# Five loads of K issued from GpSimd over part of the DMA engines, in an attention backward for one query

## The chip, the cores and the metric

The kernel runs on one core of a Trainium2 chip. The core has TensorE (PE in the profile, its weight loads PEld), VectorE (DVE), ScalarE (ACT), GpSimd (POOL) and SyncE (SP), and sixteen DMA engines that move data between the chip's DRAM and its SBUF. The metric is the time of the device in microseconds (us), from launch to end. The profile's span, from the first to the last instruction, is a little shorter than that.

## The reference

There are 32 heads. Each has one query row q of 128 numbers, and K and V of 8192 rows of 128. All are bf16. What is computed is the forward result and the three gradients of it:

```python
scores = einsum('bhqd,bhkd->bhqk', q, k) * scale
attn = softmax(scores, axis=-1)
out = einsum('bhqk,bhkd->bhqd', attn, v)
# outputs: out, and the gradients of q, k and v for the given grad_out
```

For one head, with the probabilities p (8192 numbers), dk is the outer product of ds and q, and dv is the outer product of p and grad_out. So K and V (2 MB each) are read once per head, and dk and dv (2 MB each) are written once per head: 8 MB a head, 268 MB in all. The arithmetic is small beside that.

## The kernel before: the parts concerned

A tile of K or V has 128 partitions. Partition p holds the rows 64p to 64p+63, which lie in one piece of 16 KB in DRAM. "Row" below, as in the words for this change, means such a piece of 16 KB, the share of one partition.

```python
CH = 16
K_BUFS = 3
V_BUFS = 2
NST = 2
# ...
def load_k(h):
    Kt[h] = kpool.tile([P, NT, D], BF16, tag="K", name="Kt")
    parts = NCH if h == 0 else 1
    for c in range(parts):
        nc.sync.dma_start(slots(Kt[h], c, parts), rows_of(k, h, c, parts))

def load_v(h):
    Vt[h] = vpool.tile([P, NT, D], BF16, tag="V", name="Vt")
    parts = NCH if h in (0, H - 1) else 1
    for c in range(parts):
        nc.sync.dma_start(slots(Vt[h], c, parts), rows_of(v, h, c, parts))
# ...
def outer(h, which, r):          # a quarter of dk or dv; two quarters make one store of 1 MB
    # ... nc.vector.tensor_tensor(...)
    if r % (4 // parts) == 4 // parts - 1:
        c = r // (4 // parts)
        nc.sync.dma_start(rows_of(dst, h, c, parts), slots(G, c, parts))
```

All transfers are issued from SyncE, in program order. In the loop over heads, one pass works on K and V of head h and finishes dk and dq of head h-1. The loads stand in it as follows:

```python
for h in range(H + 1):
    p_ = h - 1
    if h < H:
        # ... k_blocks (VectorE transposes of K), k_scores
        if 0 < h < H - 1:
            load_v(h + 1)
    if h > 0:
        ds_of(p_)
        outer(p_, "dk", 0)
        dq_of(p_, 0)
    # ...
    if h > 0:
        dq_of(p_, 1)             # the last use of K of head h-1
        outer(p_, "dk", 1)
    if 0 < h and h + 2 < H:
        load_k(h + 2)            # into the buffer that K of head h-1 had
    # ... softmax, outer(p_, "dk", 2), outer(p_, "dk", 3)
    # ... v_transposes, contract, v_scores
    # ... outer(h, "dv", 0) to outer(h, "dv", 3)
```

Six large transfers are issued per head: V, a store of dk, K, a store of dk, and two stores of dv.

Of the kernel before, what the change touches and what calls it, by code (L numbers as in the profile page):

```python
# [11 lines left out]
BF16 = mybir.dt.bfloat16  # L12
# [6 lines left out]
V_BUFS = 2  # L19
NST = 2  # L20
QD = 32


@with_exitstack
def kernel(
# [11 lines left out]
    nc = tc.nc  # L37
    P = 128
    _, H, S, D = k.shape
    assert D == P and S % (P * CH) == 0 and H <= P  # L40
    NT = S // P
    NCH = NT // CH
    NQ = P // QD
    assert NCH == 4 and NQ == 4
    W = D // 2
    NB = W // QD
    scale = float(D) ** -0.5
# [7 lines left out]
    small = ctx.enter_context(tc.tile_pool(name="small", bufs=2))  # L55
# [5 lines left out]
    Kt, Vt, XK, XV, st = {}, {}, {}, {}, {}  # L61

    def rows_of(x, h, c, parts):
        L = NT // parts
        return x[0, h].rearrange("(p n) d -> p n d", p=P)[:, c * L:(c + 1) * L, :]

    def slots(X, c, parts):
        L = NT // parts
        return X[:, c * L:(c + 1) * L, :]

    def load_k(h):
        Kt[h] = kpool.tile([P, NT, D], BF16, tag="K", name="Kt")
        parts = NCH if h == 0 else 1
        for c in range(parts):
            nc.sync.dma_start(slots(Kt[h], c, parts), rows_of(k, h, c, parts))

    def load_v(h):
        Vt[h] = vpool.tile([P, NT, D], BF16, tag="V", name="Vt")
# [4 lines that stand above are left out]
    rows = consts.tile([H, 2, D], BF16)  # L83
    nc.sync.dma_start(rows[:, 0, :], q.rearrange("b h s d -> (b h s) d"))
    nc.sync.dma_start(rows[:, 1, :], grad_out.rearrange("b h s d -> (b h s) d"))
    load_k(0)
    load_v(0)
    load_k(1)
    load_v(1)

# [7 lines left out]
    nc.vector.reduce_sum(in_quad[:], ident[:].rearrange("p (a i) -> p a i", a=NQ), axis=AX.X)  # L98
    lane = consts.tile([P, QD], F32)
    nc.vector.reduce_sum(lane[:], ident[:].rearrange("p (a i) -> p i a", a=NQ), axis=AX.X)  # L100
# [3 lines left out]
    for w in range(NB):  # L104
        for e2 in range(2):
            four = consts.tile([H, NQ, QD], BF16, tag=f"four{w}{e2}")
            nc.vector.tensor_copy(
                four[:], rows[:, 0, :].rearrange("h (w j e) -> h w e j", w=NB, e=2)[:, w, e2:e2 + 1, :]
                .to_broadcast([H, NQ, QD]))
            tp = psT.tile([P, CH, P], BF16, tag="T")  # L110
# [7 lines left out]
    nc.tensor.transpose(tp[:, 0, 0:H], rows[:, 1, :], ident[0:H, 0:H])  # L118
    nc.vector.tensor_copy(doT[:], tp[:, 0, 0:H])
    nc.vector.tensor_copy(do_f[:], doT[:])  # L120

    o_all = consts.tile([P, H], F32)
    dq_all = consts.tile([P, H], F32)
# [4 lines left out]
    def k_blocks(h, u):  # L128


        if u == 0:
            XK[h] = ktpool.tile([P, CH, NB, NCH, QD], F32, tag="XK", name="XK_sb")
        nc.vector.transpose(XK[h][:, :, :, u, :],  # L133
# [94 lines left out]
    for h in range(H + 1):  # L228
# [18 lines left out]
        if 0 < h and h + 2 < H:  # L247
            load_k(h + 2)
# [88 lines left out]
```

## Time and profile before

| what | value |
|---|---|
| time, median of 3 | 668.17 us (668.0 to 668.48) |
| span of the profile | 667.0 us |
| PE busy | 516.8 us, 77% |
| DVE busy | 512.5 us, 77% |
| ACT busy | 182.1 us, 27% |
| POOL busy | 0.7 us, 0% |
| read from DRAM, written to it | 134.23 MB, 134.23 MB |
| mean rate over the span | 403 GB/s |

A busy share is a mean over the span. The page of the profile also has the span in 40 equal slices, with a row for the DMA engines (tenths of busy time, mean of the sixteen) and one for what they moved in GB/s. The chain is the work that ended last, followed back from the last instruction, at each step to what released it. A line of the chain has its start, how long it took and what it was. A line of the waits has who waited, for what, for how many us in total, how many times, and the longest time. "Landing" is the moment at which a transfer's semaphore has its full count.

### The profile page before, as it was taken

What the parts mean: (1) busy time and instruction counts of PE and PEld (TensorE: products, weight loads), DVE (VectorE), ACT (ScalarE), POOL (GpSimd) and SP (SyncE); (2) the same over time, 40 slices, a digit from 0 to 9 for tenths busy, and PEclk for the clock granted to TensorE, in tenths of its full rate; (3) what the DMA queues carried; (4) which work ended last, traced back from release to release, by engine and by line L of the source; (5) the groups of instructions that cost most, each with busy time, mean ns of one, the idle gap of its engine ahead of it and who ended that gap; (6) DMA issues with size and microseconds to landing.
All of it is one profiled execution on the core that took longest, in us unless ns stands there. A gap on an engine that the chain in (4) does not pass through costs nothing.

```text
span 667.0 us, 23105 instructions
## 1 busy us (share of the span) xinstructions
PE 516.8 (77%) x10727; PEld 485.8 (73%) x10727; DVE 512.5 (77%) x658; ACT 182.1 (27%) x321; POOL 0.7 (0%) x6
## 2 busy tenths in 40 slices
PE   2887988888887777878779787787776888778881
PEld 1887878878877767877668676677766777677870
DVE  4797888888877797777877778777788776887762
ACT  0333323232323222232222322223312223223230
POOL 0000000000000000000000000000000000000000
PEclk9995556566565565555555655666557665555555
DMA  8999999999999999999999999999999999999783
GB/s 330 414 425 424 419 427 414 424 423 426 425 425 424 425 425 424 425 429 423 423 427 426 423 416 422 413 412 418 395 423 418 397 416 406 409 420 403 270 357 142
DMA packets 29807, 269.94 MB, mean 405 GB/s; under 512 B 3472, under 2 KB 3472, under 8 KB 6032
## 3 DMA queue, kind: packets, MB, share of 16 engines
q1 hardware_dynamic: 29712, 268.48, 97.0%
q8 instruction: 83, 1.36, 0.7%
q14 instruction: 12, 0.10, 0.0%
HBM read 134.23 MB, written 134.23 MB: 403 GB/s over the span
## 4 chain that ended last, share of the span: by engine, by line
DMA 75%; PE 17%; DVE 3%; ACT 2%; issue 1%; SPq 0%; ACTq 0%
DMA Kt<-in_k_dram 26%; DMA Vt<-in_v_dram 26%; DMA out_dram<-G_dv 23%; PE T_ps L168 7%; PE s_ps L145 2%; PE dp_ps L185 2%; PE m_ps L185 2%; PE dp_ps L180 1%; DVE XK_sb L133 1%; ACT XT_sb L170 1%; PE m_ps L255 1%; DVE G_dk L195 1%; PE m_ps L268 1%; PE s_ps L161 0%; ACT qd L211 0%
## 5 line engine op out<-in xcount | busy, mean ns | idle before, releaser
L168 PE MATMUL T_ps<-ident,Vt 128*128 128x128 bf16 x2048 | 228.7, 302 | 31.9 <-DMA Vt<-in_v_dram 31.9
L168 PEld LDWEIGHTS <-Vt 128*128 128x128 bf16 x2048 | 201.1, 142 | 33.8 <-DMA Vt<-in_v_dram 33.6
L133 DVE STREAM_TRANSPOSE XK_sb<-Kt 128x1024 f32<-128x1024 f32 x128 | 148.2, 1213 | 81.1 <-DMA Kt<-in_k_dram 81.1
L170 ACT COPY XT_sb<-T_ps 128x1024 f32<-128x1024 f32 x128 | 129.5, 1012 | 189.7 <-PE T_ps L168 189.7
L195 DVE TENSOR_TENSOR G_dk<-ds_rep,qd 128x2048 bf16<-128x2048 bf16 x128 | 155.7, 1219 | 1.1
L195 DVE TENSOR_TENSOR G_dv<-p_rep,qd 128x2048 bf16<-128x2048 bf16 x128 | 148.2, 1220 | 8.5 <-ACT p_rep L277 8.5
L180 PEld LDWEIGHTS <-XT_sb 128*128 128x128 bf16 x2048 | 74.7, 106 | 27.2 <-ACT XT_sb L170 27.2
L180 PE MATMUL dp_ps<-doT,XT_sb 128*128 128x1 bf16 x2048 | 73.6, 166 | 24.4 <-ACT XT_sb L170 24.4
L145 PE MATMUL s_ps<-q_blk,XK_sb 128*128 128x4 bf16 x2048 | 59.1, 168 | 23.2 <-DVE pdt L216 20.5
L145 PEld LDWEIGHTS <-XK_sb 128*128 128x128 bf16 x2048 | 56.5, 103 | 25.5 <-DVE pdt L216 22.3
L185 PE MATMUL dp_ps<-ds_rep,Kt 128*128 128x1 bf16 x2048 | 64.7, 165 | 6.6 <-issue 6.0
L185 PEld LDWEIGHTS <-Kt 128*128 128x128 bf16 x2048 | 59.9, 104 | 12.3 <-issue 12.3
L185 PEld LDWEIGHTS <-Vt 128*128 128x128 bf16 x2048 | 61.1, 105 | 0.0
L185 PE MATMUL m_ps<-p_rep,Vt 128*128 128x1 bf16 x2048 | 60.5, 166 | 0.0
L226 ACT COPY dq_all<-dp_ps 128x1 f32<-128x1 f32 x32 | 5.1, 159 | 173.9 <-PE dp_ps L185 173.9
L268 PEld LDWEIGHTS m_ps<-rs,ones_f 128*128 128x128 f32 x64 | 16.0, 310 | 48.6 <-ACT e L267 48.6
L268 PE MATMUL m_ps<-rs,ones_f 128*128 128x1 f32 x64 | 18.7, 360 | 39.2 <-ACT e L267 39.2
L264 DVE TENSOR_REDUCE nbias<-m_ps 128x1 f32<-128x128 f32 x32 | 9.3, 292 | 22.0 <-ACT qd L211 22.0
L255 PE MATMUL m_ps<-diag,ones_f 128*128 128x128 f32 x64 | 25.3, 499 | 0.7 <-DVE diag L253 0.7
L218 DVE SCALAR_TENSOR_TENSOR ds_rep<-dp_ps,pdt,p_s 128x256 bf16<-128x256 f32 x32 | 15.5, 484 | 12.0 <-PE dp_ps L180 9.6
L277 ACT ACTIVATE p_rep<-e,rinv 128x256 bf16<-128x256 f32 x32 | 16.2, 507 | 30.3 <-DVE rinv L275 30.3
L211 ACT CAST qd<-m_ps 128x256 bf16<-128x256 f32 x32 | 11.9, 372 | 42.4 <-PE m_ps L207 42.4
(40 smaller groups left out, 163.0 us busy)
## 6 DMA issues: line engine op xcount, KB each, us to landing
Kt<-in_k_dram SPq DMA_DIRECT2D x31, 2048.0 KB, 28.0
out_dram<-G_dv SPq DMA_DIRECT2D x62, 1024.0 KB, 25.8
out_dram<-G_dk SPq DMA_DIRECT2D x62, 1024.0 KB, 28.0
Vt<-in_v_dram SPq DMA_DIRECT2D x30, 2048.0 KB, 28.3
Vt<-in_v_dram SPq DMA_DIRECT2D x8, 512.0 KB, 13.8
Kt<-in_k_dram SPq DMA_DIRECT2D x4, 512.0 KB, 5.4
out_dram<-G_dv SPq DMA_DIRECT2D x4, 512.0 KB, 16.9
out_dram<-G_dk SPq DMA_DIRECT2D x4, 512.0 KB, 10.7
```

The costliest lines, as they stand in the source:

```text
L133: nc.vector.transpose(XK[h][:, :, :, u, :], slots(Kt[h], u, NCH).rearrange("p g d -> p (g d)").bitcast(F32).rearrange("p (g w j) -> p g w ...
L145: nc.tensor.matmul(out[:, g, :], lhsT=cols[:, g, c // 2, c % 2], rhs=q_blk[:, h, c, :], start=(c == 0), stop=(c == 2 * NB - 1), skip_group ...
L168: nc.tensor.transpose(T_ps[:, i, :], Vt[h][:, c * CH + i, :], ident[:])
L170: nc.scalar.copy(X.rearrange("p c s -> p (c s)").bitcast(F32), T_ps.rearrange("p c s -> p (c s)").bitcast(F32))
L180: nc.tensor.matmul(st[h]["dp"][:, n:n + 1], lhsT=X[:, i, :], rhs=doT[:, h:h + 1], start=True, stop=True, skip_group_check=True)
L185: nc.tensor.matmul(out_col, lhsT=Xt[:, n, :], rhs=rep[:, n, 0:1], start=(n == 0), stop=(n == NT - 1), skip_group_check=True)
L195: nc.vector.tensor_tensor(slots(G, r, 4).rearrange("p n (a b) -> p n a b", b=R), slots(rep, r, 4).unsqueeze(2).to_broadcast([P, Q, D // R, ...
L211: nc.scalar.copy(x["qd"][:].rearrange("p a d -> p (a d)"), x["m"][:, 256:512])
L218: nc.vector.scalar_tensor_tensor(out=x["ds"][:], in0=x["dp"][:, 0:NT].unsqueeze(2).to_broadcast([P, NT, R]), scalar=pdt[:], in1=x["p_s"][: ...
L255: nc.tensor.matmul(x["m"][:, 128:256], lhsT=ones_f[:], rhs=diag[:], start=True, stop=True, skip_group_check=True)
L268: nc.tensor.matmul(x["m"][:, 0:1], lhsT=ones_f[:], rhs=rs[:], start=True, stop=True, skip_group_check=True)
L277: nc.scalar.activation(x["p"][:], e[:].unsqueeze(2).to_broadcast([P, NT, R]), ACT.Copy, scale=rinv[:])
```

## The change

Five of the 32 loads of K (heads 5, 11, 17, 23 and 29) are cut in two. The first 120 partitions are loaded by a transfer issued from GpSimd, the last 8 by one issued from SyncE. The aim is that 15 of the sixteen DMA engines carry the 120 partitions, 8 each[...]. To choose the engine that is left out, a small load of 5 rows of 256 bytes into an unused tile is issued from GpSimd at the start, and another of one such row after each of the five loads. [...] What is computed stays the same.

```diff
+SHIFT = 4
+SHIFTED = (5, 11, 17, 23, 29)
@@
     def load_k(h):
         Kt[h] = kpool.tile([P, NT, D], BF16, tag="K", name="Kt")
+        if h in SHIFTED:
+
+            own = k[0, h].rearrange("(p n) d -> p n d", p=P)
+            nc.gpsimd.dma_start(Kt[h][0:P - 8], own[0:P - 8])
+            nc.sync.dma_start(Kt[h][P - 8:P], own[P - 8:P])
+            turn_cursor(1, h)
+            return
         parts = NCH if h == 0 else 1
         for c in range(parts):
             nc.sync.dma_start(slots(Kt[h], c, parts), rows_of(k, h, c, parts))
+
+    def turn_cursor(n, h):
+        pad = small.tile([SHIFT + 1, D], BF16, tag="pad", name="pad")
+        nc.gpsimd.dma_start(pad[0:n], k[0, h, 0:n, :])
@@
     nc.vector.tensor_copy(do_f[:], doT[:])
+
+    turn_cursor(SHIFT + 1, 0)
```

## The prediction

> **What bounds the kernel now.** I read the page's row of slices and its queues first, then the stretches of time, then the chain that ended last, then the waits of the queue that issues the transfers. The slices and queues:
>
> ```profile
> DMA  8999999999999999999999999999999999999783
> GB/s 330 414 425 424 419 427 414 424 423 426 425 425 424 425 425 424 425 429 423 423 427 426 423 416 422 413 412 418 395 423 418 397 416 406 409 420 403 270 357 142
> q1 hardware_dynamic: 29712, 268.48, 97.0%
> q8 instruction: 83, 1.36, 0.7%
> ```
>
> The sixteen DMA engines are busy to the end of the 36th slice, at 425 GB/s in the first half and at 395 to 420 later. No compute engine reaches that: PE and DVE are busy 77%. In the middle stretch the chain is transfers and nothing else:
>
> ```profile
> 432.42 28.04 DMA Kt<-in_k_dram
> ...
> 460.52 26.15 DMA out_dram<-G_dv
> ...
> 486.73 28.32 DMA Vt<-in_v_dram
> ...
> 515.12 28.36 DMA Kt<-in_k_dram
> ```
>
> Each took 26 to 28 us from issue to landing, although 2 MB at 425 GB/s are 4.9 us: the transfers stand in a queue. How long the queue may be is told by the waits of the issuing queue in 340 to 620 us:
>
> ```profile
> SPq L203 <- DMA out_dram<-G_dk: 59.1, 26, 2.5
> SPq L203 <- DMA Kt<-in_k_dram: 58.8, 13, 5.2
> SPq L75 <- DMA Vt<-in_v_dram: 58.2, 13, 4.5
> SPq L81 <- DMA out_dram<-G_dv: 34.0, 15, 2.9
> SPq L203 <- DMA out_dram<-G_dv: 32.8, 13, 2.6
> ```
>
> A transfer isn't held up by its data but by the landing of an older transfer. Eight semaphores go round, so the ninth transfer waits until the first has landed on all its engines.
>
> The averages hide one thing. The trace has, for each transfer, the sixteen increments of its semaphore, one for each DMA engine; they have no engine's number, but they have times. At 81 us the last of the sixteen comes 4 us after the first, at 205 us 9.7 us, at 345 us 17.5 us, and from 415 to 635 us always 20 to 22 us. The last but one is 9 to 13 us ahead of the last; the other fourteen lie in front of it. So one engine is slower than fifteen, and falls back about 1 us a head until the others have used up the window of eight and must wait for it: from there on all go at its pace, which is the fall from 425 to about 410 GB/s. Between 150 and 600 us the last increments of successive transfers are 4.90 us apart for a load of 2 MB and 2.72 us for a store of 1 MB. That engine never rests: even the last stores come 1.2 us (512 KB) apart on it, and its last increment is at 666.05 us, where the others have posted theirs by 659.7 us. So the end of the kernel is one engine's sum of work. A row of K is 16 KB and the engine has 8 of a load's 128 rows: one row costs it 4.90 / 8 = 0.612 us.
>
> [...]
>
> **The change part by part.** (1) Five loads of K (h = 5, 11, 17, 23, 29) lose rows 0 to 119 to GpSimd. If 15 engines with 8 rows each carry them, one engine has none. (2) [...]5 x 1 x 0.612 = +3.1 us there. (3) [...] Six more small transfers; they are on no path that anything waits for. (4) GpSimd issues when the K buffer is free, without waiting for the window of eight, and its queue runs beside SyncE's. K then comes early and a V load in the other queue up to 4.9 us later; the sum of an engine's work is the same, and with 20 us of queue on the slow engine nothing runs dry. I count 0[...].
>
> What decides is which engine is left out. [...]
> As intended: 5 x (8 - 1) = 35 rows off it, 35 x 0.612 = -21.4 us. But then the second-slowest sets the pace. It is 12.6 us ahead when the last K lands (626.5 us); it may have up to 5 rows more, 3.1 us. So that landing comes 10 to 12.6 us earlier; and the 6.3 us by which the slow engine ends last go too. Sum: -16 to -19, 668.2 - 17.5 = 650.7 us.
> By the exception: [...]+3.1 us, 671.2 us.
> [...]-1.8 us, 666.3 us.
>
> **The rivals.** These three are rivals to each other, and none of the 21.4 us can be had by more than the first. For the first speaks that 35 rows x 0.612 is nearly the lag of 20 to 22 us, so that the number looks chosen from such a trace. [...] A fourth: the loads from GpSimd cost more than they shift, [...]because two queues share an engine badly; then 675 us and above. Against it, only 5 of the 32 loads of K are concerned, and GpSimd can issue them earlier than SyncE, which stands in line for its window. A fifth: compute takes the bound. Against it, the stretches:
>
> ```profile
> 130.00:340.00 210.00, 171.87 (x3517) 162.15 (x3515) 166.94 (x208) 60.70 (x105) 0.00 (x0) 0.54 1.01 425
> 340.00:620.00 280.00, 215.10 (x4522) 201.38 (x4523) 216.60 (x275) 74.90 (x135) 0.00 (x0) 0.57 1.00 412
> ```
>
> The columns are us, then busy us of PE, weight loads, DVE, ACT and GpSimd, the granted clock, DMA's share and GB/s. In 340 to 620 us PE is busy 77% and DVE 77%; a gain of 3% of the pace leaves room.
>
> **Range and chances.** As intended 0.30 (648 to 655 us); exception 0.43 (669 to 674); cursor not turned by the small pad 0.15 (665 to 668); something between or an added cost 0.12. The middle of these is 669 us, and that is the prediction; the range of 649 to 674 us must hold the first case too. More than 2% faster is under 654.8 us: most of the first case, 0.27. More than 2% slower is over 681.5 us, the fourth rival at its worst: 0.05. Within 2%: 0.68.
>
> **What would show it.** The sixteen increments of each transfer are the measure. As intended: after each shifted load the last of the sixteen draws closer to the rest by 4.3 us, the lag stays under about 12 us, and the rate stays near 425 GB/s past 340 us. By the exception: the lag grows as before to 20 to 22 us, one engine of the fast ones gains 5 us of lead, and the last load lands 3 us later. [...] GpSimd's cost would show as a K landing from GpSimd that comes later than 28 us after its issue and as DVE idle time before the transposes of just these heads. The prediction is wrong [...]if its slowness isn't in its sum of work but goes over to another engine when it is relieved.

## The result, and the profile after

| kernel | median | lowest to highest, runs |
|---|---|---|
| before, on the same chip | 668.09 us | 667.7 to 668.48, 4 |
| changed | 695.18 us | 694.8 to 696.16, 4 |

The ratio is 1.0408, with a 95% interval of 1.039 to 1.0426: 27.1 us slower, 5.4 us for each of the five shifted loads. The span grows from 667.0 to 693.1 us. The bytes moved are the same but for the pads.

The slices and queues of the page after:

```profile
DMA  8999999999999999999999999989999999899893
GB/s 328 422 417 422 335 380 424 426 421 427 425 323 414 423 425 425 425 426 363 351 406 427 426 426 425 414 283 382 410 425 425 424 425 304 335 382 424 333 366 138
...
q1 hardware_dynamic: 29072, 258.65, 91.3%
q0 software_dynamic: 912, 9.83, 5.1%
q8 instruction: 84, 1.38, 0.8%
```

The row of DMA says nearly what it said before: busy everywhere. The row of GB/s doesn't. It has five dents, at slices 5, 12, 19 to 20, 27 and 34 to 35, down to 283 to 363 where most of the rest is near 425. A slice is 17.3 us, and GpSimd issues its five loads between 72.6 and 572.3 us, about 125 us apart: one dent for each. The queue q0 is GpSimd's. It moved 9.83 MB, 3.7% of the bytes, and took 5.1% of the engines' time. So busy engines move less.

The stretches around the first shifted load show it more sharply. First the changed kernel, then the kernel before in the middle one of these stretches. The columns are us, busy us of PE, weight loads, DVE, ACT and GpSimd, the granted clock, DMA's share and GB/s:

```profile
60.00:76.00 16.00, 14.02 (x279) 13.21 (x277) 13.62 (x19) 4.64 (x9) 1.05 (x2) 0.50 1.02 427
77.00:90.00 13.00, 10.45 (x269) 10.19 (x267) 10.93 (x13) 4.17 (x5) 0.00 (x0) 0.63 1.00 258
95.00:107.00 12.00, 10.77 (x190) 10.26 (x187) 10.99 (x14) 4.54 (x9) 0.00 (x0) 0.54 1.01 417
```

```profile
77.00:90.00 13.00, 11.38 (x283) 11.05 (x280) 11.84 (x15) 3.52 (x6) 0.00 (x0) 0.63 1.00 418
```

DMA's share stays at 1.00 while the rate goes from 427 to 258 GB/s and back to 417. The kernel before has 418 there. The data that this stretch lacks is 13 x (418 - 258) = 2.1 MB, which at 425 GB/s is 4.9 us. The load itself is 120 rows x 16 KB = 2 MB: the loss is about as large as if it had taken twice its time.

The chain of waits that ended last, its pieces that lie beside the second to the fifth shifted load:

```profile
184.76 36.45 DMA Vt<-in_v_dram
...
311.95 37.83 DMA Vt<-in_v_dram
...
441.09 37.03 DMA Vt<-in_v_dram
...
568.62 39.52 DMA Vt<-in_v_dram
```

These loads of V took 36 to 40 us, where a piece of the chain before took 26 to 28. The waits of the queue that issues the transfers, whole run:

```profile
SPq L218 <- DMA out_dram<-G_dk: 136.0, 54, 10.5
SPq L218 <- DMA Kt<-in_k_dram: 110.8, 27, 13.0
```

In the kernel before:

```profile
SPq L203 <- DMA out_dram<-G_dk: 111.7, 52, 2.5
SPq L203 <- DMA Kt<-in_k_dram: 110.8, 26, 5.2
```

The longest single waits are 10.5 and 13.0 us; before, the same two had 2.5 and 5.2. The sums tell less (the first one grows by 24.3 us, the second one is 110.8 us in both kernels); the longest one points to the harm, because it is in five places.

The DMA issues of the changed kernel:

```profile
Vt<-in_v_dram SPq DMA_DIRECT2D x30, 2048.0 KB, 28.0
Kt<-in_k_dram SPq DMA_DIRECT2D x26, 2048.0 KB, 26.0
Kt<-in_k_dram POOLq DMA_DIRECT2D x5, 1920.0 KB, 20.1
```

The shifted loads land 20.1 us after their issue, sooner than a load of K from SyncE. Read alone, this line says that they are the good ones. They are in nobody's queue but their own; what they take is taken from the transfers beside them.

### The profile page after: what moved, and what is told of

It reads as the page before. It is cut to its first block, busy times and chain, and to the rows that moved or that the text cites. A ratio compares the mean times of both kernels' runs of the same rounds, so it can differ in the third digit from the quotient of the medians.

```text
span 693.1 us, 23139 instructions
## 1 busy us (share of the span) xinstructions
PE 511.3 (74%) x10727; PEld 481.1 (69%) x10727; DVE 512.2 (74%) x658; ACT 182.5 (26%) x321; POOL 6.5 (1%) x17
## 3 DMA queue, kind: packets, MB, share of 16 engines
q0 software_dynamic: 912, 9.83, 5.1%
## 4 chain that ended last, share of the span: by engine, by line
DMA 73%; PE 19%; DVE 2%; issue 2%; ACT 2%; SPq 0%; ACTq 0%
DMA Vt<-in_v_dram 37%; DMA Kt<-in_k_dram 21%; DMA out_dram<-G_dv 15%; PE T_ps L183 9%; PE m_ps L200 2%; PE s_ps L160 2%; PE dp_ps L195 2%; PE dp_ps L200 2%; DVE XK_sb L148 1%; ACT XT_sb L185 1%; PE m_ps L270 1%; DVE G_dk L210 1%; PE m_ps L283 1%; PE m_ps L299 0%; PE s_ps L176 0%
## 5 line engine op out<-in xcount | busy, mean ns | idle before, releaser
L183 PE MATMUL T_ps<-ident,Vt 128*128 128x128 bf16 x2048 | 224.5, 298 | 25.3 <-DMA Vt<-in_v_dram 23.7
L183 PEld LDWEIGHTS <-Vt 128*128 128x128 bf16 x2048 | 198.2, 140 | 26.8 <-DMA Vt<-in_v_dram 25.1
L200 PEld LDWEIGHTS <-Kt 128*128 128x128 bf16 x2048 | 59.9, 104 | 17.4 <-issue 17.3
L200 PEld LDWEIGHTS <-Vt 128*128 128x128 bf16 x2048 | 61.1, 105 | 0.0
## 6 DMA issues: line engine op xcount, KB each, us to landing
Kt<-in_k_dram POOLq DMA_DIRECT2D x5, 1920.0 KB, 20.1
```

What stands on the lines that cost most here:

```text
L183: nc.tensor.transpose(T_ps[:, i, :], Vt[h][:, c * CH + i, :], ident[:])
L200: nc.tensor.matmul(out_col, lhsT=Xt[:, n, :], rhs=rep[:, n, 0:1], start=(n == 0), stop=(n == NT - 1), skip_group_check=True)
```

## The experiments

The first theory after this reading, the one that the first four expectations were written with, was the second queue: two queues with work on the same engines at once cost the rate. Its rivals: a load of 120 partitions, spread over 15 engines, goes at half the rate, whoever issues it; a load from GpSimd is slow in itself beside a busy VectorE; the pads or the 8-row tail cost. The first two runs refuted the second queue, and the spread became the theory. The two kernels of stages ran once each. All other times are medians with lowest, highest and number of runs; ratios are to the kernel before, run on the same chip.

### Five whole loads from GpSimd, and from ScalarE

```diff
-            nc.gpsimd.dma_start(Kt[h][0:P - 8], own[0:P - 8])
-            nc.sync.dma_start(Kt[h][P - 8:P], own[P - 8:P])
-            turn_cursor(1, h)
+            nc.gpsimd.dma_start(Kt[h][:], own)      # second kernel: nc.scalar
-    turn_cursor(SHIFT + 1, 0)
```

> The five loads go to GpSimd whole: 128 rows on all sixteen engines, no tail from SyncE, no pads. If the loss comes from two queues with work on the same engines at once (theory), it stays: 690 to 700 us, and about 280 GB/s while the load from GpSimd runs. If it comes from 15 engines with 8 rows each, or from the tail and the pads (rival), it goes: 666 to 672 us.

> The five loads go whole to ScalarE's queue in place of GpSimd's. If any second queue beside SyncE's costs the rate (theory in its wide form), 690 to 700 us. If only GpSimd's queue does[...] (theory in its narrow form), 666 to 671 us.

From GpSimd 666.07 us (665.46 to 666.44, 8), ratio 0.9969 (0.9958 to 0.9979). From ScalarE 666.11 us (665.35 to 667.42, 14), ratio 0.9974 (0.9967 to 0.9982). The 690 to 700 us of the first theory did not come. Neither costs anything; both gain 0.3%, for a reason that no run settles. One stretch of the kernel that loads from GpSimd, in the time of its first such load:

```profile
77.00:85.00 8.00, 7.25 (x118) 7.16 (x115) 6.93 (x8) 3.20 (x4) 0.00 (x0) 0.57 0.99 416
```

416 GB/s, with DVE busy 6.93 of 8 us and GpSimd's queue and SyncE's running together. So the second queue and a slowness of GpSimd's own loads fall as causes. In its DMA issues:

```profile
Kt<-in_k_dram POOLq DMA_DIRECT2D x5, 2048.0 KB, 15.4
```

15.4 us to landing for 128 rows, 20.1 for 120: 4.7 us more for less data. By an estimate from the prediction's 0.612 us a row, that is about what eight rows on an engine take (8 x 0.612 = 4.9).

### The same spread from SyncE alone

```diff
-            nc.gpsimd.dma_start(Kt[h][0:P - 8], own[0:P - 8])
+            nc.sync.dma_start(Kt[h][0:P - 8], own[0:P - 8])
             nc.sync.dma_start(Kt[h][P - 8:P], own[P - 8:P])
-            turn_cursor(1, h)
-    turn_cursor(SHIFT + 1, 0)
```

> 120 rows and then 8 rows, both from SyncE, no GpSimd and no pads. One queue alone, but 15 engines with 8 rows each. If two queues are the cause: 668 to 673 us[...]. If the spread of 120 rows is the cause: 690 to 700 us.

705.7 us (704.1 to 706.64, 4), ratio 1.0562 (1.054 to 1.0584). The loss is there without GpSimd, without a second queue and without pads. The time lies above the 690 to 700 us expected of it. A stretch of it:

```profile
82.00:90.00 8.00, 4.62 (x154) 4.47 (x151) 5.66 (x8) 1.96 (x2) 0.00 (x0) 0.69 1.01 241
```

241 GB/s beside a DMA share of 1.01, as in the changed kernel. It loses 37.7 us, 2.1 us a load more than the changed kernel does. Here each shifted head puts two transfers into SyncE's window of eight, where the changed kernel puts one; whether this is the cause wasn't tried.

### Stages of loads alone, without the attention

This kernel leaves out all of the attention, and its outputs are neither computed nor written. It has one stage after another, most of them waiting for the one before: a load from one issuer or loads from several side by side (`sp` SyncE, `pl` GpSimd, `act` ScalarE; `q` is 120 rows).

```python
stage("sp",   [(sp, 128, ld)])
stage("spq",  [(sp, q, ld)])
stage("pl",   [(pl, 128, ld)])
stage("plq",  [(pl, q, ld)])
stage("qq",   [(sp, q, ld), (pl, q, ld)])    # its GpSimd load began during "plq"
stage("spsp", [(sp, 128, ld), (sp, 128, ld), (sp, 128, ld)])
stage("sppl", [(sp, 128, ld), (pl, 128, ld), (sp, 128, ld)])
stage("spplq", [(sp, 128, ld), (pl, q, ld), (sp, 128, ld)])
```

> No attention at all: a row of stages with 2 MB loads and stores that compute nothing, each stage after the one before has landed. A load alone from SyncE 5 to 7 us[...]. Three loads of 2 MB side by side: 15 us if all are from SyncE; if one is from GpSimd, 20 us or more by the theory, 15 to 17 us by the rivals; if one is from ScalarE, 20 us or more by the wide form of it, 15 to 16 us by the narrow form. 120 rows from SyncE beside 120 from GpSimd: if both leave the same engine out, fifteen engines do all of it, 10 us or more.

From a load's issue to its landing, the longest of the stage, from the trace:

```
                                   128 rows   120 rows
one load, SyncE                      7.7 us    11.8 us
one load, GpSimd                     8.1 us    12.2 us
SyncE, GpSimd, SyncE side by side   17.0 us    22.2 us
three from SyncE                    16.6 us
```

The stretches with 128 rows from GpSimd alone, with 120 rows from GpSimd, and with three whole loads from SyncE (the columns are us, DVE, GpSimd, clock, DMA share, GB/s):

```profile
32.00:36.00 4.00, 0.00 (x0) 0.00 (x0) 1.00 0.98 414
41.00:49.00 8.00, 0.00 (x0) 0.00 (x0) 1.00 0.93 199
72.00:86.00 14.00, 0.34 (x2) 0.00 (x0) 1.00 0.99 424
```

GpSimd in place of SyncE adds 0.4 us a load, alone or beside the others. 120 rows in place of 128 add 4.1 us alone and 5.2 us between two whole loads. With a whole load from GpSimd in the middle the 17.0 us lie where the rivals had them (15 to 17), not at the 20 us or more of the second queue. Two stages were not clean and are not used: one with a ScalarE load in the middle took 18.0 us, but a store of the next stage ran beside it; and the GpSimd load of "qq" was issued 0.5 us after that of "plq", so it stood in the same queue behind it during the stretch of 199 GB/s. The single load from SyncE (11.8 us) has nothing beside it.

### Which partitions: stages of two loads

Again without the attention, outputs not computed. Two transfers side by side in each stage, over the partitions named:

```python
stage("all",   [(sp, 0, 128, ld), (sp, 0, 128, ld)])
stage("low",   [(sp, 0, 64, ld), (sp, 0, 64, ld)])
stage("mid",   [(sp, 32, 96, ld), (sp, 32, 96, ld)])
stage("midq",  [(sp, 32, 92, ld), (sp, 32, 92, ld)])
stage("midpl", [(pl, 32, 92, ld), (pl, 32, 92, ld)])
stage("q",     [(sp, 0, 120, ld), (sp, 0, 120, ld)])
stage("st",    [(sp, 0, 128, st), (sp, 0, 128, st)])
stage("stq",   [(sp, 0, 120, st), (sp, 0, 120, st)])
# then "left", "leftpad", "leftafter": 120 rows from SyncE and 120 from GpSimd,
# the second with a pad of 5 rows from GpSimd behind them
```

> No attention: stages of two loads or two stores side by side, rows of 16 KB, each stage after the last. Theory: [...]what counts is which partitions, not how many engines. Then 64 rows from partition 0 run at half the rate of 64 rows from partition 32 (about 215 against 400 GB/s in the middle of the stage), 60 rows from partition 32, which are 15 engines, run nearly as fast as 64 from there, from GpSimd as from SyncE, and a store of 120 rows takes about twice a store of 128. Rival (15 engines or an odd number of them are slow as such): 64 rows run fast from either place, and 60 rows are slow. For the engine left out: if GpSimd leaves out the same engine as SyncE, with and without pads before it, none of SyncE's fifteen landings comes early beside GpSimd's load[...].

The two stores of "st" did not wait: they were issued 0.4 us after the second load of "q" and stood in SyncE's queue behind both. One stretch from each of the first eight stages, in this order, same columns:

```profile
12.00:20.00 8.00, 0.16 (x1) 0.00 (x0) 1.00 1.01 434
24.00:32.00 8.00, 0.16 (x1) 0.00 (x0) 1.00 1.06 217
37.00:40.00 3.00, 0.16 (x1) 0.00 (x0) 1.00 1.02 426
45.00:48.00 3.00, 0.16 (x1) 0.00 (x0) 1.00 0.92 382
53.00:56.00 3.00, 0.16 (x1) 0.00 (x0) 1.00 0.95 399
71.00:78.00 7.00, 0.00 (x0) 0.00 (x0) 1.00 0.97 204
80.00:88.00 8.00, 0.22 (x3) 0.00 (x0) 1.00 0.96 410
92.00:100.00 8.00, 0.00 (x0) 0.00 (x0) 1.00 0.92 225
```

Sixty-four partitions from 0 go at 217 GB/s, sixty-four from 32 at 426: same bytes, same 16 engines, half the rate. Sixty partitions from 32, on 15 engines (DMA share 0.92 and 0.95), go at 382 (SyncE) and 399 (GpSimd), near 15/16 of 426 = 399. So 15 engines are not the loss. 120 partitions from 0 go at 204, and two such loads land 9.66 us apart where whole ones land 4.88 apart. A store has the same loss, 225 against 410.

The stage "q" also shows that its loads leave one engine out. Of the sixteen increments of the first store behind them one comes at 65.63 us and the other fifteen at 84.15 to 84.93: one engine had no load before it. The 410 GB/s of the stores, in 80 to 88 us, are thus the rate of the other fifteen.

Why these partitions make the difference is not shown. The trace names no engine of a transfer, so it doesn't tell which engine moved which rows. And no stage moved the rows in DRAM without the partitions, so whether the loss lies on SBUF's side or on DRAM's is open too.

In the last three stages SyncE's and GpSimd's 120 rows ran side by side. Fifteen increments of each SyncE load lie within 1 us (124.75 to 125.75 in "left"); an engine of SyncE's that GpSimd had left out would have come several us before the rest (such a load lands 12.1 us after its issue in "q", with no other load before it, and 15.8 us after it here). So both leave out the same engine, with the pad and without.

### The change without its pads

```diff
-            turn_cursor(1, h)
-    turn_cursor(SHIFT + 1, 0)
```

> The change without its six pads. If the pads play no part (theory: the same engine is left out with or without them), as the change: 693 to 698 us. If the pads cost, or choose the engine, it differs by 3 us or more.

695.6 us (694.64 to 696.17, 4), ratio 1.0405 (1.039 to 1.0421), against 695.18 with them. The pads neither cost anything nor change anything.

### Is it one engine that is slow? Extra rows in the kernel before

```diff
+    def extra(h):
+        t = xpool.tile([EXTRA, NT, D], BF16, tag="X", name="extra")
+        nc.sync.dma_start(t[:], k[0, h].rearrange("(p n) d -> p n d", p=P)[0:EXTRA])
@@
+            if h % 3 == 1:
+                extra(h)
```

Ten extra loads of 4 rows, or of 5 rows, into an unused tile. The trace has four, or five, increments of data for each of them. The author expected 667 to 670 us if the extra rows miss the slow engine and 673 to 675 us if one row of each load falls on it.

> The kernel before, and ten more loads of 4 rows of 16 KB from SyncE that nothing reads: [...]6.1 us of work on each of them. [...]these four have that to spare: 667 to 670 us. [...]673 to 675 us.

> The same with 5 rows[...]. [...]673 to 675 us. [...]667 to 670 us, as with 4 rows.

With 4 rows 668.06 us (667.65 to 668.91, 12), ratio 0.9998 (0.999 to 1.0007). With 5 rows 676.88 us (676.24 to 677.26, 4), ratio 1.0125 (1.0108 to 1.0142). Forty extra rows, four to a load, cost nothing; ten more, one to a load, cost 8.8 us. The increments of the extra loads say the same without the time. The four rows of the load issued at 393.50 us land between 403.66 and 406.65; of the five rows of that issued at 398.60 us, four land between 404.92 and 410.06 and the fifth at 425.30, 15.2 us behind. So a load of 5 rows reaches the slow engine and one of 4 rows does not. The engine's number is not in the trace. Ten rows at 0.612 us are 6.1 us; where the other 2.7 come from wasn't tried.

### One shifted load

`SHIFTED = (17,)`, else the change as it is.

> The change with one shifted load (head 17) in place of five. Theory: every shifted load costs the slow engine 8 rows at twice the time and one row from the tail, 8 x 0.61 + 0.61 = 5.5 us: 673 to 674 us. If the cost is not per load (rival: one thing at the start, or only what piles up over several loads), 668 to 670 us or near 695 us.

672.66 us (671.67 to 672.8, 4), ratio 1.0065 (1.0048 to 1.0081): +4.3 us, where five cost 5.4 each. The cost is there with one load already; why the single one costs 1 us less is open.

### All later loads of K from GpSimd, whole

`SHIFTED = tuple(range(2, 32))`, with the body of the first experiment. If five gain 0.3%, thirty might gain more.

> All thirty later loads of K whole from GpSimd, 128 rows each, no tail and no pads. If a load of 128 rows from GpSimd is as good as one from SyncE (theory): 655 to 668 us. If [...]a second queue cost something that five loads didn't show: 672 us or more.

675.19 us (674.6 to 676.77, 4), ratio 1.0111 (1.0094 to 1.0128). A miss: it is slower. Its DMA issues, and the waits of TensorE for V and of VectorE for the products of V:

```profile
Kt<-in_k_dram POOLq DMA_DIRECT2D x30, 2048.0 KB, 14.1
Vt<-in_v_dram SPq DMA_DIRECT2D x30, 2048.0 KB, 31.3
PE T_ps L180 <- DMA Vt<-in_v_dram: 57.7, 21, 6.1
DVE ds_rep L230 <- PE dp_ps L192: 88.6, 32, 5.9
```

The same lines of the kernel before:

```profile
Kt<-in_k_dram SPq DMA_DIRECT2D x31, 2048.0 KB, 28.0
Vt<-in_v_dram SPq DMA_DIRECT2D x30, 2048.0 KB, 28.3
PE T_ps L168 <- DMA Vt<-in_v_dram: 31.9, 21, 2.1
DVE ds_rep L218 <- PE dp_ps L180: 9.6, 9, 1.5
```

K lands in 14.1 us instead of 28.0, V in 31.3 instead of 28.3, and both waits that need V grow. The reading is that the early landing of K was taken from V, which is needed next; no run puts V first instead.

### The slow engine left out

The same change with another pattern of memory: the 120 rows in two transfers of 2 x 4 KB a partition, so that the pattern has a second dimension of more than one element (below: one that counts). The pads have one too: one of 5 rows at the start, one of 17 behind each transfer and one of 11 at the end. They are meant to make the slow engine the one that each shifted load leaves out.

```diff
-SHIFTED = (5, 11, 17, 23, 29)
+SHIFTED = (11, 23)
@@
-            nc.gpsimd.dma_start(Kt[h][0:P - 8], own[0:P - 8])
+            four = own[0:P - 8].rearrange("p (a m) d -> p a (m d)", a=4)
+            to = Kt[h][0:P - 8].rearrange("p (a m) d -> p a (m d)", a=4)
+            for part in range(2):
+                nc.gpsimd.dma_start(to[:, part::2], four[:, part::2])
+                turn_cursor(17)
@@
-            turn_cursor(1, h)
@@
-        pad = small.tile([SHIFT + 1, D], BF16, tag="pad", name="pad")
+        pad = small.tile([17, 2, 64], BF16, tag="pad", name="pad")
@@
+    turn_cursor(16 - SHIFT - 1)         # at the end
```

Three kernels: this one with two shifted loads; the same without the pads of 5 and 11; this one with all five, which is the change as it was meant. The first expectation has 661 to 667 us if the slow engine is left out of both loads, and 677 to 681 us if it is a fast one, as in the change; the last one has 648 to 655 us if to leave the slow engine out is worth what the prediction said.

> Two shifted loads (heads 11 and 23), each of them two transfers from GpSimd whose access pattern counts along two dimensions (120 partitions and two pieces of 4 KB), after a pad of 5 such rows; a pad of 17 rows after each[...]. [...]saves 2 x 7 x 0.61 = 8.6 us, the others lose 2 x 4.9 us or so and become the bound: 661 to 667 us. [...]2 x 5.4 us more, 677 to 681 us.

> The same two loads without the pad of 5 rows at the start[...]: 677 to 681 us by both readings. If it is as fast as the one with the pad, something other than the engine left out makes those loads cheap.

> Five loads[...]: the change as it was meant. If the half rate makes the other engines the bound (theory): they get 5 x 4.9 us more each, and the next slowest was 12.6 us ahead, so 676 to 684 us. [...]648 to 655 us.

| kernel | median (range, runs) | ratio, 95% |
|---|---|---|
| two loads, with the pad of 5 | 665.01 us (664.63 to 666.52, 4) | 0.9959 (0.9944 to 0.9975) |
| two loads, without the pads of 5 and 11 | 673.32 us (672.85 to 674.46, 4) | 1.0082 (1.0067 to 1.0097) |
| five loads, with the pad of 5 | 671.08 us (670.1 to 671.47, 4) | 1.0042 (1.0025 to 1.0059) |

With this pattern a pad of 5 rows makes 8.3 us of difference. The increments show where. With the pad, over the first of the two loads the last increment, 3.2 us behind the last but one, comes to 0.3 us behind. Without it, one fast engine has 3.5 us of lead after that load, as one has 5.5 in the change, and the slow one falls back as before: between 420 and 600 us the median distance from the last but one to the last is 10.9 us, against 10.7 in the kernel before and 1.4 with the pad. So in this pattern the pad of 5 rows decides which engine is left out, and with it that is the slow one. In the pattern of the change the pads had no such effect (695.6 without them against 695.18 us). The two patterns differ in the second dimension that counts, but also in the size of a piece (16 and 4 KB) and the number of transfers, and which of these matters was not tried apart.

The kernel without the pad of 5 misses its expectation: 677 to 681 us were expected, and it costs +5.0 us, 2.5 a load, less than half of the 5.4 of the change. So the price of a shifted load isn't the same in this pattern; why is open.

With five loads the change as meant is 24.1 us faster than as written, and still 0.4% slower than the kernel before. The slow engine no longer stands alone: the median distance from the last but one to the last is 0.7 us between 420 and 600 us. The stretches of the kernel with two loads, ahead of its first shifted load and over it:

```profile
170.00:184.00 14.00, 10.12 (x218) 9.14 (x215) 12.19 (x17) 3.47 (x7) 3.40 (x4) 0.50 1.02 428
186.00:206.00 20.00, 14.67 (x318) 13.69 (x315) 13.47 (x19) 5.65 (x10) 0.00 (x0) 0.50 1.02 351
```

351 against 428 GB/s with the engines busy: the loss of rate is there for the relieved kernel also. The expectation for five loads, 676 to 684 us, took 4.9 us of loss for each load on the fifteen other engines and 12.6 us of lead for the nearest of them; at 671.08 us it is a miss. An estimate from the stretch is nearer: 20 x (428 - 351) = 1.5 MB, 3.6 us a load, 18 for five, less the 12.6 us of lead, is +5.4 us, and +3.2 was measured. That the other engines set the pace here is argued and not shown.

### The 120 rows laid over other partitions

As the kernel with two loads and the pad of 5, but the 120 rows are cut into partitions 32 to 91, 0 to 29 and 92 to 121 from GpSimd, and the eight left from SyncE. So sixty of the rows lie where the stages had 382 and 399 GB/s; no stage measured the other two pieces.

```diff
+            for a, z in ((32, 92), (0, 30), (92, 122)):
+                for part in range(2):
+                    nc.gpsimd.dma_start(to[a:z, part::2], four[a:z, part::2])
+                    turn_cursor(17)
+            for a, z in ((30, 32), (122, 126), (126, 128)):
+                nc.sync.dma_start(Kt[h][a:z], own[a:z])
```

> Two loads [...]in three pieces from GpSimd (partitions 32 to 91, 0 to 29, 92 to 121) and the last 8 rows by SyncE[...]. [...]the 60 rows from partition 32 go at the full rate, the others lose 2 x 2.4 us in place of 2 x 4.9, and it is 1 to 4 us faster than the same with 120 rows in one piece: 661 to 664 us. If pieces and pads cost more than that, 665 us or more.

664.89 us (663.66 to 664.95, 4), ratio 0.995 (0.9935 to 0.9965). Its stretch over the first shifted load:

```profile
186.00:206.00 20.00, 14.91 (x323) 13.92 (x321) 13.71 (x18) 5.14 (x9) 4.67 (x6) 0.59 1.03 376
```

376 GB/s instead of 351, but the time can't be told from the 665.01 us of the simpler kernel: the 1 to 4 us that were expected did not show, so this run doesn't show that other partitions are worth time in the kernel. Both beat the kernel before by about half a per cent; that with two loads the other engines' lead pays for the loss of rate is the author's estimate.

## Why the prediction was wrong

**What bounds the kernel: right.** The end is one engine's sum of work. Ten rows more on it cost 8.8 us, forty rows that miss it nothing. Each of the ten rows cost 0.88 us there and not the 0.612 that the prediction had for a row; that is open.

**The exception: right as to the engines.** The most likely case, at 0.43, was that a fast engine is left out each time and that the pads do nothing. After the changed kernel's first shifted load one fast engine has 5.5 us of lead, after the second 12.9, and the kernel without pads has the same time. The slow engine isn't relieved: its gap to the next one grows from 0.2 to 3.6 us between 109 and 188 us. So the case of 665 to 668 us, in which the first load alone relieves it, fails as well.

**The failed step.** It is part (4), "the sum of an engine's work is the same" and "I count 0", and with it the sum of the case "By the exception", "+3.1 us". Both priced a row of the shifted load at 0.612 us, a row's share in a load of 128 rows. In a load of 120 rows a row costs twice that, 1.21 us (two loads land 9.66 us apart instead of 4.88). An estimate with the measured term is 5 x (4.78 more for the rows + 0.612 for the tail) = 27.0 us; measured +27.1. So close a fit is partly luck: the same sum gives 5.4 us for the single load, which cost 4.3, and for a load from SyncE alone, which cost 7.5. What the runs show is that the spread of 120 rows brings the loss of rate; what a load costs by it differs from kernel to kernel, from 2.5 us (two loads without the pad of 5) to 7.5. The working went from rows to engines and never asked whether a row costs the same in a load over other partitions.

**The case "as intended": wrong as well.** It promised -16 to -19 us. With the slow engine really left out the five loads give +3.2 us, and two give -3.3. The loss of rate stays in these kernels (351 against 428 GB/s); that it falls on the other fifteen engines and uses up their lead is the estimate above, not shown by a run of its own. The prediction gave the second-slowest engine up to 5 rows more, 3.1 us, and no loss of rate.

**The fourth rival: right in its size, wrong in its reason.** It had "675 us and above", and 0.05 for more than 681.5 us, for loads from GpSimd that cost more than they shift, as when two queues share an engine badly. The whole loads from GpSimd (666.07 us) and ScalarE (666.11 us) refute that for five loads. That the measured time lies in its range is luck.

**What would show it.** The sign set for GpSimd's cost, a landing later than 28 us after the issue, did not come: 20.1 us. The cost was there all the same, in the rate of everything beside it. The better sign would have been GB/s against DMA's share over the shifted load.

## What to carry to other kernels

Where DMA's share stays at 1 and GB/s falls (here 1.00 and 427 to 258), look at the partitions that the transfers cover: a transfer over fewer than 128 need not be a shorter copy of the whole one (120 from 0 at 204 GB/s, 128 at 434), and a stage of two such loads (9.66 against 4.88 us) shows the loss before the kernel is rebuilt around it. Taking work off the slowest of many engines is worth at most what the others can take on, and here the new shape cost rate as well (351 against 428 GB/s), so begin with one or two transfers and not with five. And a transfer that lands early in its own queue may have taken its time from one that is needed sooner (K 14.1 instead of 28.0 us, V 31.3 instead of 28.3).

## What the runs showed of the hardware that was not expected

- 120 partitions from 0 move at 204 GB/s as a load and 225 as a store, against 434 and 410 for 128; 64 partitions from 32 move at 426 and from 0 at 217.
- One of the sixteen engines is slower in this kernel than the others: ten extra loads of 5 rows cost 8.8 us, ten of 4 rows nothing, and one row of a five-row load lands 15.2 us behind the other four. Why it is slower is open.
- Whether a pad from GpSimd changes which engine is left out went with the pattern: the pads changed nothing with one dimension that counts (695.6 us without them, 695.18 with), and the pad of 5 rows 8.3 us with two (665.01 against 673.32). The two patterns differ in more than that.
- A second queue cost nothing for five loads (ratios 0.9969 and 0.9974) and 1.1% for thirty.
